# Turning double-precision weights into single precision: the lowest three fraction bits by ScalarE through PSUM, one VectorE operation in place of two, and a new written order

## The chip, the cores and the metric

The kernel runs on one core of one Trainium2 chip. The metric is the device time of one execution in microseconds. A core has five engines that work side by side, each through its own queue in order: TensorE (PE in the profile; its weight loads are PEld), VectorE (DVE), ScalarE (ACT), GpSimd (POOL) and SyncE (SP), which here starts most of the transfers.

## The reference, cut to what matters

Three layers follow one another. Attention keeps, for each query, the 32 largest of 576 scores. A dense layer multiplies by `w_in`, takes h cos(h), and multiplies by `w_out`. A layer of 8 experts sends each token to the expert with the largest logit.

```python
scores = scale * np.matmul(q, k.transpose(0, 1, 3, 2))     # 2 x 8 heads, 576 x 576
kth = np.partition(scores, -32, axis=-1)[..., -32:-31]
scores = np.where(scores >= kth, scores, -1e9)
attn = exp(scores - max); attn /= attn.sum + 1e-09
x = np.matmul(attn, v)                                      # as 1152 tokens x 512
h = x @ w_in;  x = (h * np.cos(h)) @ w_out                  # 512 x 2048, 2048 x 512
expert = argmax(x @ w_gate)                                 # 8 experts, capacity 288
out[i] = gate[i] * (relu(x[i] @ w1[expert]) @ w2[expert])
```

`w_in` and `w_out` come in double precision (their scale is a numpy double), all else in single precision. TensorE needs single precision, so the kernel builds the single-precision words itself from the two 32-bit halves of each double.

## The kernel before, in words

The program is a list of 3678 small operations. Each is registered with `P.op(engine, cost, function, r=..., w=...)`: the cost is a price in us that only the planner uses, `r` and `w` name the tiles read and written. `P.flex` registers an operation with two or three engines to choose from; the string `PICKS` holds the choice for the first 612 of them. `ORDER` is a written permutation of all 3678. The planner walks through it (`in_order`), gives every new tile a slot of its ring, and issues the instructions, so `ORDER` is the order of each engine's queue. Waits between engines come from the tiles that the instructions really touch; `r` and `w` only set what may be issued when.

Attention goes in 36 steps, 32 whole ones of 128 queries for a pair of heads and 4 of another shape. In a whole step TensorE computes the scores in two halves of 288 columns into the single PSUM buffer `S`; each half is copied to `Sp` in SBUF (`scores`, L665 on ScalarE or L666 on VectorE). The fold (`pair_chain`, L835) takes the elementwise maximum and minimum of the two halves, the second read from `S`, the first from `Sp`; then VectorE draws the largest eight three times from the maxima (L847, L850) and once from all (L854), the last one ending the step's list. `softmax` subtracts a penalty (L892), exponentiates (L895) and scales (L905 to L907); `products` transposes (copies L665, L666) and multiplies with the values.

The doubles lie as pairs of 32-bit words. `convert` handles them in 32 chunks of 128x512: 16 of `w_in`, 16 of `w_out`. A first pass (L692 on ScalarE, L693 on GpSimd) scales the upper word, read as a float, which moves the exponent. VectorE shifts it left by three (L697, L707) and puts in the top three bits of the lower word (L699, L709). The sign is put back by VectorE for the first three chunks (L702), and by a ScalarE sign (L706) and a GpSimd product (L712) for the other 29.

The dense layer takes token tiles as their steps end (`layer_in`, `cosine`, `product`, `layer_out`). The sums of `layer_out` for one token tile stand in a PSUM tile `x2`, a ring of two slots. `route` and `place` find each token's expert and slot, with operations of 8 or fewer elements a partition; `largest` tallies (L1217 to L1225) and counts doubtful decisions (L1235 to L1237). Last come the experts, on TensorE mostly, each weight rounded and its remainder subtracted (`weights2`).

Of the kernel before, what the change touches and what calls it, by code (L numbers as in the profile page):

```python
# [11 lines left out]
I32 = mybir.dt.int32  # L12
U32 = mybir.dt.uint32
# [26 lines left out]
SIGN = -2 ** 31  # L40
HALF_PI = 1.5707964
# [5 lines left out]
    "1000000000000000000000000000000010000000000000000200000000000000000000000000000110000100000001000100"  # L47
    "0010000000010000000000000100000000010100000000000100000002000000000210000000001001000010000000100000"
    "0000000000000000000022000100000110000002000000022000000022010000001000000010000001122000000010000101"
    "0011110001201110111111110000001010010000010000000101100000000000000000000010110101111101110100100101"  # L50
    "0101100000000111011101111101010000001000000000000000100110110111010000000110000000101001001000011011"
    "0001010000010101001011100100100110001111111101001010000000000101101000000010110101110011110110010001"
    "000000000000")
ORDER = [
# [490 lines left out]
def forward(ctx, lasting, tc, kq, vn, vs_, w_in, w_out, w_gate, w1, w2, out, paired):  # L545
# [125 lines left out]
    def convert(n):  # L671
# [9 lines left out]
        def half():  # L681
            return T[kt][:, 0]

        def full():
            return T[kf]
# [87 lines left out]
    ring("pt", "ps", [128, 512], F32, 2)  # L773
    ring("av", "ps", [128, 512], F32, 1, tag="av")
    ring("h", "pa", [128, 512], F32, 1)
    ring("x2", "ps", [128, 512], F32, 2)
    ring("xn", "xq", [128, 4, 128], F32, 2, tag="xl")

    def load_kq(s):
# [874 lines left out]
```

## Time and profile before

| | us |
|---|---|
| median of 3 runs | 663.94 (662.0 to 667.82) |
| the profiled execution | 664.33 |
| its span | 662.4 |
| busy in the span: TensorE | 583.6 (88%) |
| VectorE | 557.3 (84%) |
| ScalarE | 484.3 (73%) |
| GpSimd | 318.1 (48%) |

The span runs from the first to the last instruction of one execution. Busy time is the sum of the times in which an engine executes; register, branch and semaphore instructions don't count. The shares are averages over stages with different limits. The mean granted clock of TensorE is 0.963 of full speed.

### The profile page before, as it was taken

How to read it: one execution, taken by the hardware profiler on the slowest of the kernel's cores; microseconds unless marked ns; L12 is line 12 of the kernel's file. 1: busy time of each engine (PE TensorE's matmuls, PEld its weight loads, DVE VectorE, ACT ScalarE, POOL GpSimd, SP SyncE). 2: the span in 40 equal slices, each digit the busy share in tenths (PEclk: the TensorE clock that was granted, in tenths of full speed). 3: DMA queues.
4: the chain of work that ended last, by engine and by line, in shares of the span. 5: the costliest groups of instructions: out<-in, count | busy, mean ns of one | idle time of the engine just before them, and what ended most of it. 6: DMA issues, size and time to landing. Idle time of an engine off the chain costs nothing.

```text
span 662.4 us, 11583 instructions
## 1 busy us (share of the span) xinstructions
PE 583.6 (88%) x3808; PEld 452.8 (68%) x3808; DVE 557.3 (84%) x1541; ACT 484.3 (73%) x996; POOL 318.1 (48%) x406
## 2 busy tenths in 40 slices
PE   2256878888989999999999999999789999999994
PEld 0024665665447866778577688788468998889993
DVE  5999999999999999999999997556656688787782
ACT  3588798988997979979878787345336677777771
POOL 1557667777786887646666625045531010101111
PEclk9986689999999999999999999999879899999998
DMA  8756596822222243232121110242335587676750
GB/s 274 229 162 221 146 390 258 284 68 57 72 83 83 91 129 102 62 104 81 47 84 59 41 41 18 84 137 99 117 124 174 173 267 249 223 233 203 246 180 16
DMA packets 44613, 94.62 MB, mean 143 GB/s; under 512 B 7165, under 2 KB 11261, under 8 KB 44544
## 3 DMA queue, kind: packets, MB, share of 16 engines
q1 hardware_dynamic: 42800, 89.04, 41.2%
q0 software_dynamic: 1744, 4.76, 1.9%
q8 instruction: 32, 0.52, 0.3%
q14 instruction: 37, 0.30, 0.2%
HBM read 81.87 MB, written 12.69 MB: 143 GB/s over the span
## 4 chain that ended last, share of the span: by engine, by line
PE 41%; DVE 35%; issue 12%; ACT 6%; POOL 3%; DMA 1%; POOLq 0%; SPq 0%; DVEq 0%; ACTq 0%
DVE C L850 8%; DVE W L847 7%; PE yp L1503 6%; PE x L1109 5%; DVE C L835 4%; PE hp L1458 4%; PE x L1101 4%; DVE W L854 3%; PE h L1026 3%; DVE wt L709 3%; PE h L1028 2%; PE h L1027 2%; PE hp L1463 2%; PE av L936 2%; PE pt L922 2%
## 5 line engine op out<-in xcount | busy, mean ns | idle before, releaser
L892 POOL TENSOR_TENSOR Sp<-Sp,pen 128x576 f32<-128x576 f32 x62 | 82.6, 1333 | 29.5 <-ACT pen L888 27.2
L847 DVE MAX8 W<-C 128x8 f32<-128x288 f32 x216 | 93.9, 451 | 2.1
L850 DVE MATCH_REPLACE8 C<-W,C 128x288 f32<-128x288 f32 x216 | 94.7, 441 | 0.0
L807 PE MATMUL S<-kq 64*128 64x288 f32 x256 | 56.0, 519 | 33.4 <-DVE C L835 16.5
L1508 POOL DMA_INDIRECT out_dram<-ot,ti x16 | 16.1, 1004 | 140.1 <-ACT ot L1517 72.3
L1101 PE MATMUL x<-wo,hs 128*128 128x512 f32 x148 | 73.4, 606 | 1.6 <-POOL wo L712 0.8
L922 PE MATMUL pt<-ident,Sp 128*128 128x128 f32 x324 | 55.9, 294 | 16.1 <-ACT Sp L905 11.6
L922 PEld LDWEIGHTS pt<-ident,Sp 128*128 128x128 f32 x324 | 39.0, 148 | 43.3 <-ACT Sp L905 19.8
L888 ACT ACTIVATE pen<-Sp,tb 128x576 bf16<-128x576 f32 x72 | 55.4, 769 | 13.2 <-POOL tb L881 6.4
L807 PEld LDWEIGHTS S<-kq 64*128 64x128 f32 x256 | 22.1, 210 | 55.0 <-issue 30.2
L895 ACT ACTIVATE Sp<-Sp,tb 128x576 f32<-128x576 f32 x72 | 55.4, 771 | 5.3 <-POOL Sp L892 4.1
L1028 PE MATMUL h<-xh,wl 128*128 128x256 f32 x192 | 54.2, 282 | 0.0
L854 DVE MAX8 W<-C 128x8 f32<-128x576 f32 x72 | 52.7, 749 | 0.7
L665 ACT ACTIVATE Sp<-S 128x576 f32<-128x576 f32 x66 | 42.3, 641 | 14.7 <-PE S L807 9.3
L835 DVE TENSOR_TENSOR C<-S,Sp 128x576 f32<-128x576 f32 x64 | 47.5, 750 | 6.4 <-ACT Sp L665 4.4
L665 ACT ACTIVATE PT<-pt 128x384 f32<-128x384 f32 x89 | 41.6, 488 | 13.7 <-PE pt L922 10.7
L936 PE MATMUL av<-PT,v 128*64 128x128 f32 x320 | 45.6, 291 | 5.5 <-DVE xl L969 4.0
L936 PEld LDWEIGHTS av<-PT,v 128*64 128x64 f32 x320 | 36.5, 144 | 17.9 <-DVE xl L969 5.5
L938 PE MATMUL av<-PT,v 128*64 128x128 f32 x320 | 45.6, 291 | 1.8 <-DVE PT L666 1.2
L905 ACT ACTIVATE Sp<-Sp,sm 128x576 f32<-128x576 f32 x49 | 37.0, 769 | 4.8 <-DVE sm L900 4.6
L1463 PE MATMUL hp<-xgs,la 128*128 128x192 f32 (+2 forms) x160 | 40.2, 254 | 0.0
L1458 PE MATMUL hp<-xgs,wk 128*128 128x384 f32 x128 | 39.9, 374 | 0.0
(224 smaller groups left out, 1868.9 us busy)
## 6 DMA issues: line engine op xcount, KB each, us to landing
raw<-in_w_dram SPq DMA_DIRECT2D x64, 512.0 KB, 4.4
kq<-in_kq_dram SPq DMA_DIRECT2D x40, 288.0 KB, 3.4
v<-in_vn_dram SPq DMA_DIRECT2D x32, 320.0 KB, 3.4
wraw<-in_w_in_dram SPq DMA_DIRECT2D x16, 512.0 KB, 5.7
wraw<-in_w_out_dram SPq DMA_DIRECT2D x16, 512.0 KB, 4.1
xs<-z SPq DMA_DIRECT2D x1, 4680.0 KB
v<-in_vs_dram SPq DMA_DIRECT2D x8, 320.0 KB, 3.0
out_dram<-z SPq DMA_DIRECT2D x1, 2304.0 KB
```

Of the source, the lines that this page charges most:

```text
L665: P.flex([("act", act, lambda: ACT.activation(*args(), AF.Copy, scale=scale), False), ("dve", dve, lambda: DVE.tensor_scalar(*args(), scal ...
L807: PE.matmul(T[kp][:, a, 0:HS], t[p, S:S + 128], t[p, i * HS:(i + 1) * HS], start=True, stop=True)
L835: DVE.tensor_tensor(out=o[:, :, c:c + HS], in0=T["S", (s, 1)][:, :, 0:HS], in1=x[:, :, 0:HS], op=op)
L847: P.op("dve", 0.372, lambda r=r, i=i: DVE.max(T["W", s][:, i, LIST[r]:LIST[r] + 8], T["C", s][:, i, 0:HS]), r=[("C", s, i)], w=[("W", s, i)])
L850: P.op("dve", 0.42, lambda r=r, i=i: DVE.match_replace(T["C", s][:, i, 0:HS], T["W", s][:, i, LIST[r]:LIST[r] + 8], T["C", s][:, i, 0:HS], ...
L854: P.op("dve", 0.665, lambda i=i: DVE.max(T["W", s][:, i, 40:48], T["C", s][:, i, :]), r=[("C", s, i), ("C", s, 2 + i)], w=[("W", s, i)])
L892: eng.tensor_tensor(out=T["Sp", s][:, i, :], in0=T["Sp", s][:, i, :], in1=T[kp], op=OP.subtract)
L922: PE.transpose(T[kp][:, c * 128:(c + 1) * 128], P2[:, cc * 128:(cc + 1) * 128], ident)
L936: PE.matmul(o[0:64, 0:128], v[:, c * 64:(c + 1) * 64], chunk(c), start=(c == 0), stop=(c == 4), skip_group_check=True)
L1028: PE.matmul(o, lo, a, start=False, stop=(kc == 3), skip_group_check=True)
L1101: P.op("pe", 0.87, lambda f=f, a=a: PE.matmul(T["x2", t], T[kh][:, a:a + 128], T["wo", f], start=(f == 0), stop=(f == 15)), r=[kh, ("wo", ...
L1458: PE.matmul(o, hi_at(ka)[:, c:c + 128], x.rearrange("p a n -> p (a n)"), start=(kc == 0), stop=False, skip_group_check=True)
```

## The change

ScalarE gets a pass for each chunk that multiplies the lower word, read as an unsigned integer, by just under 2^-29, subtracts just under one half, and writes the result as an integer, 0 to 7, into PSUM. One VectorE operation shifts the scaled upper word and joins these bits to it, in place of two. The new tiles `lo` share the two slots of `x2`. The sign is handled as before.

```diff
+TOP3 = 2.0 ** -29 * (1 - 2.0 ** -21)
+HALF = 0.5 - 2.0 ** -21
...
+        kl = ("lo", n)
+        P.op("act", 0.5, lambda: ACT.activation(T[kl], T[kr][:, :, 0].bitcast(U32), AF.Copy, scale=TOP3, bias=-HALF), r=[kr],
+             w=[kl])
         P.flex([("act", 0.56, lambda: ACT.activation(half(), T[kr][:, :, 1].bitcast(F32), AF.Copy, scale=2.0 ** -112), False),
...
         if n < prm["mul"]:
-
-            P.op("dve", 0.34, port=True, fn=lambda: DVE.tensor_scalar(bits(full()), bits(half()), 3, None,
-                                                                      op0=OP.logical_shift_left), r=[kt], w=[kf])
-            P.op("dve", 0.60, port=True, fn=lambda: DVE.scalar_tensor_tensor(
-                bits(full()), T[kr][:, :, 0], 29, bits(full()), op0=OP.logical_shift_right, op1=OP.bitwise_or),
-                r=[kr], w=[kf])
+            P.op("dve", 0.62, port=False, fn=lambda: DVE.scalar_tensor_tensor(
+                bits(full()), bits(half()), 3, T[kl], op0=OP.logical_shift_left, op1=OP.bitwise_or),
+                r=[kt, kl], w=[kf])
...
         else:
             P.op("act", 0.56, lambda: ACT.activation(full(), T[kr][:, :, 1].bitcast(F32), AF.Sign), r=[kr], w=[kf])
-            P.op("dve", 0.34, port=True, fn=lambda: DVE.tensor_scalar(bits(half()), bits(half()), 3, None,
-                                                                      op0=OP.logical_shift_left), w=[kt])
-            P.op("dve", 0.60, port=True, fn=lambda: DVE.scalar_tensor_tensor(
-                bits(half()), T[kr][:, :, 0], 29, bits(half()), op0=OP.logical_shift_right,
-                op1=OP.bitwise_or), r=[kr], w=[kt])
+            P.op("dve", 0.62, port=False, fn=lambda: DVE.scalar_tensor_tensor(
+                bits(half()), bits(half()), 3, T[kl], op0=OP.logical_shift_left, op1=OP.bitwise_or),
+                r=[kl], w=[kt])
...
-    ring("x2", "ps", [128, 512], F32, 2)
+    ring("x2", "ps", [128, 512], F32, 2, tag="x2")
+    ring("lo", "ps", [128, 512], I32, 2, tag="x2")
...
-                P.op("dve", 0.69, lambda c=c, op=op: fold(c, op, 0), r=[("Sp", s, 0), ("S", (s, 1))], w=w, port=False)
+                P.op("dve", 0.69, lambda c=c, op=op: fold(c, op, 0), r=[("Sp", s, 0), ("Sp", s, 1), ("S", (s, 1))], w=w, port=False)
...
-        P.op("dve", 0.4, address, r=[kp, kx + (1,), ("pick", t)], w=[("slot", t)])
+        P.op("dve", 0.6, address, r=[kp, kx + (1,), ("pick", t)], w=[("slot", t)])
...
-        P.op("dve", 0.9 if paired else 0.3, tally, r=[kp, ("slot", 8)], w=[("counts", 0)])
+        P.op("dve", 2.9 if paired else 0.9, tally, r=[kp, ("slot", 8)], w=[("counts", 0)])
...
-        P.op("dve", 0.4, lambda: (DVE.tensor_scalar(edge, edge, 0.0, 0.0, op0=OP.is_gt, op1=OP.add, accum_out=doubts[:, 0:1]),
+        P.op("dve", 4.0, lambda: (DVE.tensor_scalar(edge, edge, 0.0, 0.0, op0=OP.is_gt, op1=OP.add, accum_out=doubts[:, 0:1]),
```

The fold's `r` now names the copy of the second half, so the planner may issue a fold only after that copy; the fold itself is the same. `address`, the tally and the doubts only get other prices. `PICKS` and `ORDER` are written anew, whole. Counted over the whole program, the new `PICKS` give:

| operation | engine: before to after |
|---|---|
| first pass of a chunk | ScalarE 25 to 11, GpSimd 7 to 21 |
| copy of scores | ScalarE 66 to 61, VectorE 6 to 11 |
| penalty subtraction | GpSimd 62 to 68, VectorE 10 to 4 |
| scaling of probabilities | ScalarE 49 to 40, VectorE 10 to 14, GpSimd 13 to 18 |
| copy of transposed probabilities | ScalarE 89 to 94, VectorE 19 to 14 |
| remainders of `w_in`, `w_out` (`split_w`, `split_wo`) | GpSimd 21 to 26, VectorE 5 to 0 |
| remainder `gl` in `product` | GpSimd 10 to 14, VectorE 8 to 4 |

In the new `ORDER` the steps come in the same sequence, 20 of the 32 chunks (before 18) are joined when step 5's list ends, and all 32 (before 31) when step 12's ends.

## Rows read from the trace of the kernel before

**Rows 1.** Busy time by stretch: length, PE, PEld, DVE, ACT, POOL, PEclk, DMA share, GB/s
```profile
0.00:167.90 167.90, 114.79 (x737) 77.36 (x738) 157.50 (x401) 133.98 (x249) 105.18 (x137) 0.92 0.63 209
100.00:150.00 50.00, 44.00 (x314) 31.03 (x314) 48.81 (x124) 46.17 (x88) 37.67 (x43) 1.00 0.57 199
167.90:406.90 239.00, 229.37 (x1635) 168.21 (x1635) 225.29 (x653) 201.28 (x380) 158.69 (x206) 1.00 0.24 73
406.90:600.00 193.10, 185.63 (x1139) 159.28 (x1135) 132.74 (x369) 112.39 (x276) 47.77 (x57) 0.96 0.50 167
```
**Rows 2.** Timeline of VectorE: start, duration; the end of step 13's list
```profile
167.15 0.75 DVE L854 MAX8 W<-C 128x8 f32<-128x576 f32 x1
```
**Rows 3.** Groups by line and form, VectorE, `convert`: busy us, mean ns, idle before
```profile
L709 DVE SCALAR_TENSOR_TENSOR wt<-wraw,wt 128x512 int32<-128x512 int32 x29 | 23.2, 810 | 0.0
...
L707 DVE TENSOR_SCALAR wt<-wt 128x512 int32<-128x512 int32 x29 | 17.1, 602 | 0.0
...
L699 DVE SCALAR_TENSOR_TENSOR ws<-wraw,ws 128x512 int32<-128x512 int32 x3 | 2.3, 777 | 0.0
...
L697 DVE TENSOR_SCALAR ws<-wt 128x512 int32<-128x512 int32 x3 | 1.3, 446 | 2.2 <-ACT wt L692 2.2
```
**Rows 4.** The same view, VectorE, the fold
```profile
L835 DVE TENSOR_TENSOR C<-S,Sp 128x576 f32<-128x576 f32 x64 | 47.5, 750 | 6.4 <-ACT Sp L665 4.4 <-PE S L807 0.3
...
L837 DVE TENSOR_TENSOR C<-S,Sp 128x288 f32<-128x288 f32 x16 | 6.8, 449 | 0.6 <-ACT Sp L665 0.4
```
**Rows 5.** Instructions on `wraw`: ns minimum/median/maximum, first and last start
```profile
L709 DVE SCALAR_TENSOR_TENSOR wt<-wraw,wt x29: 664/683/1754, 12.8 to 158.8; 128x512 int32<-128x512 int32 x29
L692 ACT ACTIVATE wt<-wraw x25: 643/666/815, 7.6 to 138.3; 128x512 f32<-128x512 f32 x25
```
**Rows 6.** Groups by line and form, ScalarE, copies out of PSUM
```profile
L665 ACT ACTIVATE Sp<-S 128x576 f32<-128x576 f32 x66 | 42.3, 641 | 14.7 <-PE S L807 9.3 <-DVE C L835 3.5 <-PE pt L922 1.4
...
L665 ACT ACTIVATE hs<-h 128x512 f32<-128x512 f32 x29 | 17.1, 589 | 9.2 <-PE h L1028 9.2
```
**Rows 7.** The same view: operations whose engine the picks change
```profile
L895 ACT ACTIVATE Sp<-Sp,tb 128x576 f32<-128x576 f32 x72 | 55.4, 771 | 5.3 <-POOL Sp L892 4.1 <-DVE Sp L892 1.0
...
L665 ACT ACTIVATE PT<-pt 128x384 f32<-128x384 f32 x89 | 41.6, 488 | 13.7 <-PE pt L922 10.7 <-PE av L938 2.7
...
L905 ACT ACTIVATE Sp<-Sp,sm 128x576 f32<-128x576 f32 x49 | 37.0, 769 | 4.8 <-DVE sm L900 4.6
...
L892 DVE TENSOR_TENSOR Sp<-Sp,pen 128x576 f32<-128x576 f32 x10 | 10.5, 1052 | 0.7 <-ACT pen L888 0.7
...
L906 DVE TENSOR_SCALAR Sp<-Sp,sm 128x576 f32<-128x576 f32 x10 | 9.5, 950 | 0.1
...
L693 POOL TENSOR_SCALAR wt<-wraw 128x512 f32<-128x512 f32 x7 | 5.3, 753 | 13.6 <-DMA wraw<-in_w_in_dram 9.5 <-DVE C L850 3.9
...
L666 DVE TENSOR_SCALAR Sp<-S 128x576 f32<-128x576 f32 x6 | 4.5, 744 | 3.8 <-PE S L807 3.8
```
**Rows 8.** Waits of VectorE: total us, times, longest us
```profile
DVE C L835 <- ACT Sp L665: 4.4, 11, 0.7
```
**Rows 9.** Timeline around one fold, all engines
```profile
106.94 0.76 PE L807 MATMUL S<-kq 64*128 64x288 f32 x4
...
107.80 0.64 ACT L665 ACTIVATE Sp<-S 128x576 f32<-128x576 f32 x1
...
108.47 0.76 DVE L835 TENSOR_TENSOR C<-S,Sp 128x576 f32<-128x576 f32 x1 [0.45 <-ACT Sp L665]
```
**Rows 10.** Timeline around 470 to 476 us, all engines
```profile
470.69 3.96 DVE L1237 TENSOR_TENSOR doubtb<-doubts 128x1 bf16<-128x1 f32 x1
...
470.87 3.77 POOL L657 TENSOR_TENSOR wl<-raw,wk 128x512 fp32r<-128x512 f32 x3
...
474.58 0.68 DVE L1085 TENSOR_TENSOR hs<-hs,ur 128x512 f32<-128x512 f32 x1
...
476.05 0.50 PE L1109 MATMUL x<-vh,gh 128*128 128x512 f32 x1 [2.98 <-ACT gh L660]
```

More of the change, by code (lines that the diff above doesn't have):

```diff
@@ L12 @@
 I32 = mybir.dt.int32
+U32 = mybir.dt.uint32
 U32 = mybir.dt.uint32
@@ L46 @@
 PICKS = (
[L47 to L53, printed above, removed]
-ORDER = [
[186 rows of a table removed]
+    "1100200000000000100000000000000020100000000000000200010000120000000100000000000010000010000000010000"
+    "0000000000000110101000000000000000000011000000000010100000100000000000001000200001002000010000200001"
+    "0000000000020000000002000000011000000002000000010000000021001000010000000000000000020011001022000010"
+    "0220001001210001110211111110111100001000110110011111111100000000100000000000111101110101011111110101"
+    "0101111100001111111101010111011101000000000001000000110011010010010000100100000000100111001011101001"
+    "1000000000100111110100101010000011111100011101011010000000100000001010000000010101010101010101110101"
+    "000010001000")
+ORDER = [
[186 rows of a table added]
 ]
```

372 rows, old and new, of the table ORDER are left out of this document.

## The prediction

> **What bounds the kernel now.** I first cut the span into stages and read how busy each engine is in each [rows 1]. The cut at 167.9 us is the end of the last candidate list of attention step 13 of 36 [rows 2]: by then all 32 weight chunks are converted, and everything that the change edits in `convert` lies before it. In that first stage VectorE is busy 157.5 of 167.9 us, TensorE only 114.8, ScalarE 134.0, GpSimd 105.2. VectorE sets the pace: its idle time is 10.4 us, most of it before the first data arrive. From 167.9 to the end of step 35 at 406.9 TensorE is busy 229.4 of 239.0 us and VectorE 225.3, and from there to 600 TensorE is busy 185.6 of 193.1, VectorE 132.7. So a microsecond taken from VectorE in the first stage can shift all that follows, because TensorE's later work stays the same and only starts earlier; one taken from VectorE after 168 us buys little. The question is therefore what the first stage becomes, and then a few us around 475.
>
> **The conversion.** Before, each chunk has on VectorE a shift (L707, or L697 for the first three) and a shift-and-or (L709, L699), besides the sign operation of three chunks, which stays. Their busy time is 17.1 + 23.2 + 1.3 + 2.3 = 43.9 us [rows 3]. Both leave; one join of 128x512 with one operand in PSUM comes. No row shows just that. The nearest is the fold, two inputs with one in PSUM: 0.750 us at 576 elements and 0.449 at 288 [rows 4], so 1.05 ns an element and 0.68 us at 512. The removed operation on SBUF alone has 0.664 at its fastest and 0.810 as its mean [rows 3, 5]. I take 0.68, since the fold has the same operands' places, with 0.66 and 0.81 as ends: 32 x 0.68 = 21.8, so VectorE loses 22.1 us (18.0 to 22.8). A second way to count gives less: at nearly undisturbed length (0.446, the mean of L697, and 0.683, the median of L709 [rows 3, 5]) the removed operations make 32 x 1.129 = 36.1 us, and the other 7.8 are time spent held up beside GpSimd. Should that holding-up pass to other VectorE operations, only 36.1 - 21.8 = 14.3 us are saved.
>
> The stretching shows at L709, whose longest took 1.754 us against a median of 0.683 [rows 5], and at the tiny L1237: 3.96 us for one element a partition, from 470.69 to 474.65, while GpSimd ran three subtractions from 470.87 to 474.64 [rows 10]. The Trainium skill (SBUF — State Buffer, section "SBUF: two separate sides") says that VectorE and GpSimd share a pair of SBUF ports which one instruction holds to its end, and that a VectorE operation with two SBUF inputs takes part in that. By this rule the join, with one SBUF input, stays at 0.68 beside GpSimd; without it, 0.81 and 18.0 us saved would be as likely.
>
> **ScalarE** gets 32 new passes that read every other word of the raw chunk, as L692 does (median 0.666 us [rows 5]), and write integers to PSUM. No row shows a write of ScalarE to PSUM; the ends are 0.59, the 512-element copy out of PSUM [rows 6], and 0.77, a scaling of 576 elements [rows 7]. I take 0.67: 21.4 us (18.9 to 24.6).
>
> **The picks** move work too. I counted, in the old and the new list, what stands ahead of step 13's end. VectorE: score copies 1 to 3 (+2 x 0.744), penalty subtractions 3 to 0 (-3 x 1.052), scalings 2 to 4 (+2 x 0.950) [rows 7]: +0.2. ScalarE: 14 first passes of chunks go to GpSimd (-14 x 0.666 = -9.3 [rows 5]), 6 scalings fewer (-6 x 0.769 = -4.6 [rows 7]), two exponentials and two copies of transposed probabilities stand later (-2 x 0.771 - 2 x 0.488 = -2.5 [rows 7]). With the 21.4 that is +5.0. GpSimd takes the 14 first passes (14 x 0.753 = 10.5 [rows 7]) and six softmax operations (a third of 3.77 each, as its subtractions [rows 10]: 7.5). That makes 123 us in the stage, so GpSimd keeps about a fifth of it as slack and is not the bound.
>
> **The first stage then.** VectorE needs 157.5 - 22.1 + 0.2 = 135.6 us; with the same 10.4 idle the stage would end at 146.0. ScalarE needs 134.0 + 5.0 = 139.0, and it starts at 7.6 [rows 5]. Its highest share in any 50 us was 46.17, or 92% [rows 1], since it waits in order for products and scalars of other engines. At 92%: 7.6 + 139.0 / 0.923 = 158.2. The later of the two decides: 158.2, a gain of 9.7 us. VectorE with the small saving of 14.3 us would end at 153.8, still ahead of it. So the cover that VectorE's relief needs is ScalarE's, and only half the relief comes through.
>
> **Later stages.** From 168 to 407 TensorE idles 9.6 of 239.0 us [rows 1], and the new lists leave its work as it is: I take 0, with 4 us either way for the new order. Around 475 TensorE stood 2.98 us for a rounded product of ScalarE [rows 10], which waited for the product L1085 behind L1237 in VectorE's queue. The new list puts that last product ahead of L1237, and gives the last remainder `gl` to GpSimd (1.26 us, a third of its 3.77, in place of VectorE's 0.68, taken as long as L1085 [rows 10]): a gain of 3.0 - 0.6 = 2.4, between 0 and 3. Repricing the tally and the doubts changes no instruction, so by itself it is worth nothing. Sum: -9.7 - 2.4 = -12.1 against the profiled execution's 664.3 us (span 662.4), which lies 0.4 above the median of the three runs: 652.2.
>
> **Rivals.** (1) VectorE's relief comes through whole: ScalarE runs at 98% as VectorE now does (157.5 of some 160). For it: no row says that ScalarE can't; against it: its many waits. The stage ends at 146.0, a gain of 21.9 + 2.4: 640.0. (2) The shared PSUM slots hold ScalarE. The bits' tiles use the ring `x2` of two slots, and from step 7 to step 13 one of them holds token tile 0's sums, so nine of the new passes must each wait for the join of the one before. With VectorE full, each may block ScalarE's queue (score copies and exponentials stand behind it) for one short operation and the join, 0.45 + 0.68 = 1.13 us [rows 4]: 10.2 us, in a stage where ScalarE is the later: 662.4. (3) On the slow side: the fold. It now also names the copy of the second score half, so in the new list all 32 whole-step folds stand behind that copy, 27 of them behind ScalarE; in the old one 9 did. That order costs a real wait: at 108.02 VectorE was free, the scores were in PSUM at 107.70, and the fold began at 108.47, right behind ScalarE's copy of 107.80 to 108.44 [rows 9]. The Trainium skill (PSUM — Partial Sum Buffer, section "PSUM bank collisions raise a hardware error") says that two engines may not read one bank at once, so a program has to put them in order; the trace agrees, with those 0.45 us. Eleven such waits made 4.4 us, 0.7 at the longest [rows 8]. At 0.4 each, 18 more cost 7 us, partly inside VectorE's slack. If ScalarE is so full that each fold waits for one earlier pass and the copy (0.77 + 0.64 = 1.41 us [rows 6, 7]), 27 x 1.41 - 4.4 = 33.7, less the 13.7 us that VectorE idles after 168: +20.0, 672. With two passes ahead it is 693. From about 1.4 us a fold this makes the kernel slower; I give 680 for the case.
>
> **How the numbers follow.** Forecast, 644 to 657: 0.48. Rival 1, 637 to 644: 0.20. Rival 2, or a gain eaten by fold waits of 0.4 us, 657 to 668: 0.24. Rival 3: 0.08. The range that holds eight in ten takes in both bounds of the first stage, 637 to 665. A change of less than 1% (6.6 us, 657.3 to 670.6) can't be told from none here: faster 0.68, within 0.24, slower 0.08.
>
> **What would show it.** In the profile of the changed kernel: the join near 0.68 us, 32 times; the new ScalarE pass near 0.67; step 13's last list ending near 158; ScalarE above 90% of 10 to 158 us and VectorE a few per cent lower than now; the stall at 475 gone; TensorE's idle time before 168 us shorter by some 10 us and the same after. I would be wrong if step 13 ends at 146 (ScalarE was never a bound) or beyond 165 (slots or folds), if folds wait over 1 us, or if TensorE turns out to idle after 170 us.

## The result, and the profile after

| | before | after |
|---|---|---|
| median, us | 664.18 (662.0 to 668.74, 6 runs) | 635.94 (634.24 to 636.73, 6 runs) |
| profiled execution; its span | 664.33; 662.4 | 635.66; 633.9 |

The ratio is 0.956, with a 95% interval of 0.952 to 0.959. The forecast was 652.2 with a range from 637: right in sign, and 16 us too high. Medians and ratios here and below are those of fast runs; one of fold_dep's four runs, at 703.97 us, was slow and is left out.

The span lost 28.5 us. Cut at the ends of the last lists of steps 13 and 35, as in [rows 1, 2], it lost 14.6 in the first stage (forecast 9.7), 6.4 in the middle one (forecast 0) and 7.5 behind it (forecast 2.4). Step 13 now ends with this row of VectorE's timeline (two lists of the step that follow without a gap, in one row; line numbers differ by a few between kernels, so L856 is the L854 of before):

```profile
151.90 1.40 DVE L856 MAX8 W<-C 128x8 f32<-128x576 f32 x2
```

Busy time of the changed kernel by stage, with the columns of [rows 1]:

```profile
0.00:153.30 153.30, 110.25 (x727) 73.89 (x727) 139.38 (x371) 134.19 (x253) 112.37 (x158) 0.92 0.67 227
153.30:385.90 232.60, 229.86 (x1657) 170.11 (x1653) 218.40 (x644) 201.50 (x384) 164.61 (x213) 1.00 0.25 77
385.90:633.90 248.00, 234.27 (x1431) 204.08 (x1429) 162.85 (x485) 149.10 (x371) 63.91 (x69) 0.97 0.52 169
```

In the first stage VectorE lost 18.1 us of work, ScalarE gained only 0.2 (forecast 5.0). In the middle TensorE's idle time fell from 9.6 to 2.7 us, at nearly the same busy time (229.4 and 229.9). Behind it TensorE's busy time fell by 5.2 us and its idle time by 2.3, against this row of the kernel before:

```profile
406.90:662.40 255.50, 239.46 (x1443) 207.19 (x1438) 174.56 (x488) 149.02 (x369) 54.27 (x63) 0.96 0.49 165
```

The new operations of the changed kernel (instructions on the tile `lo`: minimum, median, maximum in ns, as in [rows 5]):

```profile
L696 ACT ACTIVATE lo<-wraw x32: 612/634/742, 7.4 to 135.9; 128x512 int32<-128x512 uint32 x32
L710 DVE SCALAR_TENSOR_TENSOR wt<-wt,lo x29: 661/677/689, 13.7 to 136.7; 128x512 int32<-128x512 int32 x29
```

The join is what was forecast, 0.68 us, and never longer than 0.689, where the operation that it replaces went up to 1.754 [rows 5]. The fold waits for ScalarE's copy less than before, 3.1 us in 5 waits against 4.4 in 11 [rows 8] (waits of VectorE, whole span; L837 is the fold):

```profile
DVE C L837 <- ACT Sp L668: 3.1, 5, 0.9
```

### The profile page after: what moved, and what is told of

Its sections match the earlier page's. It is cut to its first block, busy times and chain, and to the rows that moved or that the text cites. A ratio compares the mean times of both kernels' runs of the same rounds, so it can differ in the third digit from the quotient of the medians.

```text
span 633.9 us, 11567 instructions
## 1 busy us (share of the span) xinstructions
PE 574.4 (91%) x3808; PEld 448.1 (71%) x3808; DVE 520.6 (82%) x1498; ACT 484.8 (76%) x1006; POOL 340.9 (54%) x439
## 4 chain that ended last, share of the span: by engine, by line
PE 61%; ACT 15%; DVE 14%; issue 7%; DMA 1%; POOL 1%; SPq 0%; POOLq 0%; DVEq 0%; ACTq 0%
PE yp L1505 9%; PE x L1111 7%; PE x L1103 6%; PE hp L1460 5%; PE av L938 4%; PE pt L924 4%; PE S L809 4%; PE h L1028 3%; PE hp L1465 3%; DVE C L852 3%; PE h L1030 3%; PE h L1029 3%; DVE W L849 3%; ACT Sp L897 2%; DVE C L837 2%
## 5 line engine op out<-in xcount | busy, mean ns | idle before, releaser
L894 POOL TENSOR_TENSOR Sp<-Sp,pen 128x576 f32<-128x576 f32 x68 | 88.5, 1302 | 36.0 <-ACT pen L890 35.4
L809 PE MATMUL S<-kq 64*128 64x288 f32 x256 | 55.7, 516 | 33.7 <-DVE C L837 19.7
L668 ACT ACTIVATE PT<-pt 128x384 f32<-128x384 f32 x94 | 43.9, 488 | 12.4 <-PE pt L924 12.0
L856 DVE MAX8 W<-C 128x8 f32<-128x576 f32 x72 | 52.8, 751 | 0.6
L837 DVE TENSOR_TENSOR C<-S,Sp 128x576 f32<-128x576 f32 x64 | 47.0, 749 | 5.0 <-ACT Sp L668 3.1
L938 PEld LDWEIGHTS av<-PT,v 128*64 128x64 f32 x320 | 36.9, 145 | 14.6 <-issue 4.1
L668 ACT ACTIVATE Sp<-S 128x576 f32<-128x576 f32 x61 | 39.4, 646 | 6.2 <-PE S L809 4.8
L1087 POOL TENSOR_TENSOR hs<-hs,ur 128x512 f32<-128x512 f32 x25 | 32.7, 1310 | 8.9 <-ACT ur L1078 8.8
```

Source lines behind the costliest of these rows:

```text
L668: P.flex([("act", act, lambda: ACT.activation(*args(), AF.Copy, scale=scale), False), ("dve", dve, lambda: DVE.tensor_scalar(*args(), scal ...
L809: PE.matmul(T[kp][:, a, 0:HS], t[p, S:S + 128], t[p, i * HS:(i + 1) * HS], start=True, stop=True)
L837: DVE.tensor_tensor(out=o[:, :, c:c + HS], in0=T["S", (s, 1)][:, :, 0:HS], in1=x[:, :, 0:HS], op=op)
L894: eng.tensor_tensor(out=T["Sp", s][:, i, :], in0=T["Sp", s][:, i, :], in1=T[kp], op=OP.subtract)
L938: PE.matmul(o[0:64, 0:128], v[:, c * 64:(c + 1) * 64], chunk(c), start=(c == 0), stop=(c == 4), skip_group_check=True)
```

## The experiments

Each was run beside the kernel before; the ratio is to its median there (664.2 to 666.7). The stages are cut as above, in the profiled execution of each.

| kernel | median us | ratio, 95% interval | to step 13 | 13 to 35 | rest |
|---|---|---|---|---|---|
| before | 664.18 | 1 | 167.9 | 239.0 | 255.5 |
| after | 635.94 | 0.952 to 0.959 | 153.3 | 232.6 | 248.0 |
| conv_alone | 706.57 | 1.057 to 1.071 | 179.7 | 266.8 | 258.5 |
| fold_dep | 694.90 | 1.034 to 1.047 | 172.7 | 266.3 | 257.2 |
| conv_oldfold | 666.73 | 0.998 to 1.005 | 170.1 | 239.1 | 253.3 |
| plan_alone | 667.47 | 1.002 to 1.007 | 185.6 | 230.2 | 250.9 |
| old_picks | 664.73 | 0.995 to 1.001 | 165.5 | 244.6 | 253.8 |
| fold_first | 643.88 | 0.961 to 0.971 | 156.0 | 236.4 | 249.1 |
| dve_twice | 657.44 | 0.985 to 0.993 | 171.0 | 232.6 | 248.7 |
| act_twice | 651.81 | 0.977 to 0.986 | 168.3 | 232.9 | 249.3 |
| passes_back | 638.13 | 0.955 to 0.965 | 155.3 | 232.6 | 247.4 |
| early_old | 643.84 | 0.965 to 0.974 | 160.8 | 232.7 | 248.3 |
| passes_pool | 633.70 | 0.947 to 0.956 | 151.1 | 232.6 | 248.5 |
| late_old | 652.60 | 0.977 to 0.986 | 151.8 | 244.8 | 253.4 |
| rem_old | 644.34 | 0.965 to 0.975 | 152.2 | 237.4 | 251.9 |
| soft_old | 647.64 | 0.971 to 0.980 | 151.9 | 244.3 | 249.7 |
| doubts_late | 665.86 | 0.998 to 1.004 | 169.7 | 239.0 | 255.4 |
| gl_pool | 661.43 | 0.992 to 0.999 | 169.1 | 239.0 | 251.3 |

### Which part of the change does it?

**conv_alone**: the changed code with the old lists.

```diff
 after.py
-ORDER, PICKS of the changed kernel
+ORDER, PICKS of the kernel before; each new pass ahead of its chunk's first pass
```

> The new conversion with the old order and the old picks: each new ScalarE pass stands right ahead of its chunk's first pass, the join where the shift-and-or stood. Theory 1 (the VectorE time that the conversion no longer takes is the gain): step 13's list ends near 150 us, and the kernel takes 640 to 648, most of the 28 us gained. Theory 2 (the new order and picks bring it, since the old order sends ScalarE the same first passes and 20 us more): step 13 ends at 160 or later and the kernel takes 655 to 664.

**plan_alone**: the old code with the new lists.

```diff
 before.py
-ORDER, PICKS of the kernel before
+ORDER, PICKS of the changed kernel; both old operations where the join stands
```

> The old conversion with the new order and the new picks: the shift stands right ahead of the shift-and-or, where the join stood, and no ScalarE pass writes PSUM. Theory 1: VectorE is as loaded as before, step 13 ends near 168 and the kernel takes 655 to 668, at most the few us of the stall near 475 gained. Theory 2: ScalarE is relieved by 14 first passes and 9 scalings, so that the kernel takes 640 to 648 without the new conversion.

Each half alone loses, 42 and 3 us; together they gain 28. conv_alone misses both theories: it lies 43 us above the upper end of the second. plan_alone is in theory 1's range in time, but its first stage is 18 us longer than that theory had it, and its middle one 8.8 shorter than before. The first stage of plan_alone holds 172.6 us of VectorE in 185.6, mostly because the conversion that it kept got longer. Its groups by line and form, to be laid beside L709 and L707 of [rows 3]:

```profile
L707 DVE SCALAR_TENSOR_TENSOR wt<-wraw,wt 128x512 int32<-128x512 int32 x29 | 30.0, 1035 | 1.0
L705 DVE TENSOR_SCALAR wt<-wt 128x512 int32<-128x512 int32 x29 | 20.6, 710 | 0.1
```

The same 58 instructions take 50.6 us in place of 40.3, while GpSimd runs 21 first passes in place of 7. Laid against GpSimd's rows in plan_alone's trace, the 13 shift-and-ors that ran beside no GpSimd instruction took 0.692 us on average, the 16 others 1.314. In the changed kernel the 4 joins of L710 beside none took 0.672, the 25 others 0.676. So the join lets GpSimd take work that made the old conversion longer.

The loss of conv_alone mixed two things, the conversion and the fold's new dependency, which moves 23 folds behind ScalarE's copy in the old order. Two runs take them apart.

**fold_dep**: the kernel before with the dependency.

```diff
-    fold(c, op, 0), r=[("Sp", s, 0), ("S", (s, 1))]
+    fold(c, op, 0), r=[("Sp", s, 0), ("Sp", s, 1), ("S", (s, 1))]
```

> The kernel before with one edit: the fold's list of reads names the copy of the second half too, so 23 of the 32 folds of whole steps are issued behind that copy instead of ahead of it. Conversion, order and picks are the old ones. Theory A (the dependency is the larger part of the 42 us that the conversion alone lost): each such fold waits about one pass and a copy of ScalarE (1.41 us), 23 x 1.41 = 32 us less some slack: 680 to 696 us. Theory B (it costs only where ScalarE is full, that is together with the new pass): folds wait 0.4 us each, 23 x 0.4 = 9 us at most: 664 to 673 us.

**conv_oldfold**: conv_alone without it.

```diff
-    fold(c, op, 0), r=[("Sp", s, 0), ("Sp", s, 1), ("S", (s, 1))]
+    fold(c, op, 0), r=[("Sp", s, 0), ("S", (s, 1))]
```

> The conversion of the changed kernel with the old order and the old picks, as in the run with the conversion alone, but the fold names only the copy of the first half again, so that the 23 folds which the old order has ahead of the second copy stay there. Theory A (ScalarE and VectorE both run almost without idle time): VectorE is relieved by 22 us, ScalarE's work in the first stage grows from 134.0 to 154.5 us, it starts at 7.6 and ends the stage at 162 to 166 instead of 167.9; the later stages stay as before: 657 to 664 us, folds waiting for ScalarE's copy under 6 us in total. Theory B (my prediction's share of 92%): 7.6 + 154.5 / 0.923 = 175 us for the stage, 671 us in all. Theory C (the new pass and the shared PSUM slots by themselves upset the old order, whatever the fold does): 690 us or more, as with the conversion alone, 706.

The dependency alone costs 28 us, theory A. Of the 33.8 us by which the profiled span is longer, 4.8 lie in the first stage and 27.3 between steps 13 and 35, where TensorE idles 28.2 us in place of 9.6 and its granted clock is 0.97 in place of 1.00. The waits of VectorE in fold_dep, against the 4.4 us of [rows 8]:

```profile
DVE C L835 <- ACT Sp L665: 44.1, 27, 3.5
```

The conversion without it is worth nothing, though VectorE is relieved by 19.7 us. The first stage of conv_oldfold:

```profile
0.00:170.10 170.10, 113.97 (x735) 76.57 (x736) 137.78 (x369) 149.36 (x281) 96.71 (x137) 0.91 0.60 205
```

VectorE is busy 137.8 of 170.1 us: it is no longer what holds the stage. ScalarE went from 134.0 to 149.4, and the forecast's rule (ScalarE's start, 5.8 here, and its work at 92%) gives 5.8 + 149.4 / 0.923 = 167.6; measured, 170.1 lies between theories A and B, as the time does. Its folds waited 18.4 us in all, three times what A allowed. The dependency costs 28 us without the new pass and 40 with it (conv_alone against conv_oldfold); in conv_alone the folds waited 57.2 us in all, up to 4.1.

**old_picks**: the changed kernel, old choice of engines.

```diff
 after.py
-PICKS of the changed kernel
+PICKS of the kernel before
```

> The changed kernel, its conversion and its order, with the old choice of engines: 14 first passes of chunks come back from GpSimd to ScalarE (14 x 0.666 = 9.3 us), some 9 scalings too (6 of them in the first stage, 4.6 us), and 10 remainders and 6 penalty subtractions come back from GpSimd to VectorE, most of them after the first stage. Theory A (ScalarE and VectorE both set the pace of the first stage, VectorE that of the middle one): step 13 ends 10 to 14 us later than 153.3, the middle stage gets 4 to 7 us longer than 232.6: 650 to 657 us. Theory B (the order matters and the picks don't): 636 to 640 us.

The first stage comes back by 12.2 us, as theory A had it; but the middle by 12.0, where it had 4 to 7, and the rest by 5.8, so that the time lies 8 us above its range. The picks carry all of the gain in this order. New picks in the old order were not tried, so what the order contributes by itself stays open.

**fold_first**: in the changed kernel, the second copy right behind its step's folds, in 32 steps.

```diff
-    ..., copy of the second half, ..., fold (max), fold (min)
+    ..., fold (max), fold (min), copy of the second half
-    r=[("Sp", s, 0), ("Sp", s, 1), ("S", (s, 1))]
+    r=[("Sp", s, 0), ("S", (s, 1))]
```

> The changed kernel with the fold naming only the first copy again and, in the order, the copy of the second half moved right behind the second fold of its step. All else is the changed kernel. Theory A (in the changed kernel the copy is done before VectorE comes to the fold, 3.1 us of waits in all, so the dependency costs nothing and moving the copy back can only make the buffer S free later): TensorE's scores wait longer for S, first stage 0 to 8 us longer, 636 to 644 us. Theory B (the dependency still costs about 0.4 us a fold hidden in other waits): 626 to 634 us.

Theory A, at its upper end: 8 us slower. In an order that has the copy done in time the folds wait little for it (3.1 us in the changed kernel), where the dependency cost 28 us in the old one. Moving the copy back behind the folds loses; the dependency with the order left alone was not tried.

### What holds the first stage?

**dve_twice** issues the join twice, **act_twice** the new pass twice; nothing else changes.

```diff
+    DVE.scalar_tensor_tensor(bits(half()), bits(half()), 0, T[kl], op0=OP.logical_shift_left, op1=OP.bitwise_or)
```
```diff
+    ACT.activation(T[kl], T[kr][:, :, 0].bitcast(U32), AF.Copy, scale=TOP3, bias=-HALF)
```

> The changed kernel with the join issued twice, the second time with a shift by zero, so that the result is the same: 32 more VectorE operations of 0.68 us, 21.8 us, order and picks as in the changed kernel. If VectorE still sets the pace of the first stage, step 13 ends 18 to 22 us later and the kernel takes 650 to 658. If ScalarE sets it, as the prediction had it, step 13 ends under 10 us later and the kernel takes 637 to 646.

> The changed kernel with the new ScalarE pass issued twice into the same PSUM tile: 32 more ScalarE passes of 0.64 us, 20.4 us. If ScalarE sets the pace of the first stage, step 13 ends 18 to 22 us later and the kernel takes 650 to 658. If VectorE sets it and ScalarE's 19 us of idle time take the passes in, step 13 ends under 10 us later and the kernel takes 637 to 646.

21.9 us more on VectorE (161.25 busy) make the stage 17.7 us longer, 19.1 us more on ScalarE (153.33 busy) 15.0. Both engines hold it, at four fifths of full slope each in these two profiled executions. By the medians VectorE's slope is steeper: 21.5 us for the joins, 15.9 for the passes; the profiled execution of dve_twice, 654.09, was its fastest.

**passes_back** and **passes_pool** move first passes of chunks only, **early_old** the other 25 old choices ahead of step 13's end.

```diff
-first passes: ScalarE 11, GpSimd 21
+passes_back:  ScalarE 25, GpSimd 7
+passes_pool:  ScalarE 0, GpSimd 32
```
```diff
-softmax, copies, rounding up to step 13's end: new PICKS
+early_old: old PICKS there (25 differ), first passes as in the changed kernel
```

> The changed kernel with the first passes of the chunks on their old engines: 25 on ScalarE and 7 on GpSimd in place of 11 and 21; conversion, order and all other picks are the changed kernel's. Theory A (ScalarE sets the end of the first stage, at some 92% of its time; a pass takes 0.56 us of a full queue, as the 17.8 us show that 32 doubled passes added): ScalarE's busy time there grows from 134.2 to 142, 7.6 + 142 / 0.923 = 161.5 in place of 153.3, the middle stage stays at 232.6 us and the end as it is: 642 to 646 us. Theory B (the first stage is VectorE's alone, or the order's): 635 to 638 us.

> The changed kernel with all 32 first passes of the chunks on GpSimd, 11 more than now. Theory A: ScalarE's busy time in the first stage falls from 134.2 to 128, its end by that to 7.6 + 128 / 0.923 = 146; then VectorE decides, 139.4 busy + 10.4 idle = 149.8, 3.5 us earlier than now: 631 to 634 us. Theory B (GpSimd, with 112.4 + 7.3 = 120 us of work in 150, in order, is the next to hold the chunks up): 636 to 645 us.

> The changed kernel with the old choice of engines up to step 13's last list, but not for the first passes of the chunks: 25 operations differ; ScalarE gets 15 and loses 5, some 6 us more work in the first stage, VectorE gets 7 and loses 9. Theory A (additive: all old choices made the first stage 12.2 us longer, the first passes alone 2.0): 644 to 647 us. Theory B (it takes both to fill ScalarE): 636 to 640 us.

passes_back is a miss for theory A: 7.2 us more of ScalarE cost 2.0 us. Its first stage, and that of early_old:

```profile
0.00:155.30 155.30, 109.57 (x727) 73.17 (x727) 138.82 (x371) 141.40 (x267) 104.45 (x144) 0.98 0.66 224
```
```profile
0.00:160.80 160.80, 113.24 (x728) 75.78 (x729) 138.81 (x368) 139.94 (x263) 105.86 (x151) 0.92 0.64 216
```

early_old comes out 0.2 us below theory A's range; its first stage is 7.5 us longer, where a plain sum (12.2 less 2.0) would have 10.2. It has less of ScalarE than passes_back, the same of VectorE, and ends 5.5 us later. So what counts is not the amount alone but what kind of operation moves. A likely reason, not tested by itself: first passes hang on nothing but a transfer, while softmax operations stand in a chain from one engine to the next. ScalarE's share is no constant: over the whole stage it was 87% in early_old, 87.5% in the changed kernel, 91% in passes_back and act_twice. passes_pool, in theory A's range, ends the stage 2.2 us earlier and has the lowest median of all, 633.70; its interval overlaps that of the changed kernel, so whether it is faster isn't settled.

### The middle stage

**late_old** has the old choices behind step 13's end (134 operations), **rem_old** only the eleven remainders among them, **soft_old** all but those.

```diff
-PICKS of the changed kernel behind step 13's last list
+late_old: old PICKS there
+rem_old:  old PICKS there for wl, vl (L659, L660) of w_in, w_out and gl of product
+soft_old: old PICKS there for all others
```

> The changed kernel with the old choice of engines for everything that stands behind step 13's last list in its order, and the new one ahead of it (134 operations differ: the remainders of w_in, w_out and the product that went to GpSimd come back to VectorE, with copies, scalings and products). Theory A (the later choices are what shortened the middle stage and the end): step 13 at 153.3 as in the changed kernel, the middle stage 7 to 12 us longer than 232.6, the end 3 to 6 us longer, 646 to 654 us. Theory B (the middle stage got shorter because the order changed, or because the first stage left work behind in a better state): 636 to 639 us.

> The changed kernel with only the remainders of w_in, w_out and of the dense layer's product on their old engines: 10 come back from GpSimd to VectorE and one goes the other way, all of them behind step 13. Theory A (these carry the middle stage: VectorE's 225.3 of 239.0 us there, of which the ten remainders are some 7): about two thirds of the 17 us that the run with all later choices lost, 645 to 650 us, middle stage 239 to 242. Theory B (the copies, scalings and penalty subtractions carry it): 636 to 641 us, middle stage 233 to 236.

> The changed kernel with the old choice of engines behind step 13's last list for all but those eleven remainders (123 operations). Theory A of the run with the remainders: 638 to 643 us here. Theory B: 645 to 650 us. If both this and the run with the remainders lose little (under 4 us each), the loss of 17 us comes only when both are together, that is when VectorE is full.

late_old came out in theory A's range, with the middle 12.2 us longer. Of its parts, soft_old falls where theory B had it, and rem_old between the two theories: the remainders cost 4.8 us in the middle, the other 123 choices 11.7, so the two are not a sum. All six kernels with the new later choices in the new order (the changed one, dve_twice, act_twice, passes_back, passes_pool, early_old) have 232.6 to 232.9 there, whatever their first stage was, and plan_alone, without the new conversion, has 230.2: this gain comes with the new lists, whichever conversion stands there; late_old shows that within the new order it needs the later picks. In soft_old TensorE waits where it waits in old_picks too (waits of TensorE in soft_old, 153 to 393 us):

```profile
PE pt L924 <- ACT Sp L907: 3.5, 6, 1.0
PE av L938 <- DVE xl L971: 1.2, 2, 0.8
```

These are ends of softmax chains on ScalarE and VectorE. The changed kernel has one such wait over half a microsecond there, of 0.9.

### The stall around 475

**doubts_late** moves the count of doubts, in the kernel before.

```diff
 ORDER of the kernel before
-..., doubts, last product, ..., copy xr of tile 8, ...
+..., last product, ..., doubts, copy xr of tile 8, ...
```

> The kernel before with one edit in the order: the count of doubts (VectorE, 3.96 us at 470.69) moves from ahead of the last product of the dense layer to behind it, just ahead of the copy that follows. Theory A (the stall of 2.98 us and the clock that falls with it, 0.81 in 473 to 500 and 0.93 in 500 to 550, make most of the 7.5 us by which the last part got shorter): 657 to 661 us. Theory B (my prediction's 2 to 3 us, the clock being set by other things): 661 to 663 us. Theory C (the stall moves to another wait): 664 us.

Theory C: no gain. The timeline of doubts_late, the rows of VectorE and GpSimd, shows why, beside [rows 10]:

```profile
471.04 1.67 POOL L659 TENSOR_SCALAR wk<-raw 128x512 fp32r<-128x512 f32 x2
...
472.16 4.86 DVE L1083 TENSOR_TENSOR hs<-hs,ur 128x512 f32<-128x512 f32 x1
...
472.68 3.78 POOL L655 TENSOR_TENSOR wl<-raw,wk 128x512 fp32r<-128x512 f32 x3
```

Now it is the product, 0.68 us by itself, that takes 4.86 beside the same three subtractions, while the count takes 0.16. The count was not the cause: either of these two operations, each with two SBUF inputs, is held when it stands there.

**gl_pool**: one pick, in the kernel before.

```diff
-PICKS[547] = "0"   # gl of the last product: VectorE
+PICKS[547] = "1"   # GpSimd, ahead of the three subtractions in its queue
```

> The kernel before with one pick changed: the last remainder of the dense layer's product goes to GpSimd, where it stands ahead of the three subtractions of 470.87 to 474.64 and waits for the last product by way of its rounding. So the three can't run beside the count of doubts or beside that product. Theory A (those three lengthen whatever VectorE runs beside them, 3.96 us for one element, 4.86 us for the product when the count was moved behind it): the count takes 0.2 us, the product 0.7, the stall of 2.98 us goes to under 1, and with it the lower clock behind it: 657 to 661 us, the part after step 35 at 248 to 251 us instead of 255.5. Theory B (the stall moves once more): 663 to 666 us.

Theory A in its mechanism, and 0.4 us above its range in time. The three now stand behind a remainder that waits for the last product by way of its rounding, and run when VectorE is past. VectorE and GpSimd in gl_pool's timeline:

```profile
471.87 0.22 DVE L1237 TENSOR_TENSOR doubtb<-doubts 128x1 bf16<-128x1 f32 x1
472.01 0.68 DVE L1085 TENSOR_TENSOR hs<-hs,ur 128x512 f32<-128x512 f32 x1
...
473.52 1.29 POOL L657 TENSOR_TENSOR gl<-hs,gh 128x512 fp32r<-128x512 f32 x1 [1.44 <-ACT gh L660]
474.77 3.79 POOL L657 TENSOR_TENSOR wl<-raw,wk 128x512 fp32r<-128x512 f32 x3
```

The part behind step 35 falls from 255.5 to 251.3, so this one choice is worth 4.2 of the 7.5 us in the profiled executions (3.4 by the medians). The lower clock, which theory A expected to go with the stall, stayed: 0.81 in 473 to 500 us in both kernels. rem_old agrees from the other side. With its remainders back on VectorE, the last one among them, the three subtractions run early again and hold the remainder before it, 0.69 us by itself; TensorE waits 3.0 us for that, and the part is 3.9 longer. VectorE and GpSimd in rem_old's timeline:

```profile
451.19 3.74 POOL L660 TENSOR_TENSOR wl<-raw,wk 128x512 fp32r<-128x512 f32 x3
451.29 4.21 DVE L659 TENSOR_TENSOR gl<-hs,gh 128x512 fp32r<-128x512 f32 x1 [2.00 <-POOL gh L664]
```

## Why the prediction missed, step by step

**The step that failed** is the one on the later stages: "the new lists leave its work as it is: I take 0", and 2.4 us for the stall. It holds 11.5 of the 16.4 us by which the forecast gain was too small, 6.4 in the middle stage and 5.1 behind it. The profile had the room in plain sight: 9.6 us of TensorE's idle time [rows 1], with VectorE at 225.3 of 239.0. I read TensorE at 96% as the end of the matter. I had counted the picks for the first stage only. In the new order the later ones decide there (late_old, soft_old, rem_old): with them TensorE waits less for the ends of softmax chains, and 6.9 of the 9.6 us went. What the order gives by itself stays open.

**The stall** was sized at 2.4 and measured 4.2 (gl_pool). I had named the pick that removes it and netted its price, but thought that moving the product ahead of the count was what counted; doubts_late shows that to be worth nothing. Most of the other 3.3 us shows in the granted clock, which I had not priced. These rows of the kernel before and of the changed one, with the columns of [rows 1], begin equally far behind step 35, the stall of 2.98 us left out (93.1 and 90.1 us):

```profile
500.00:550.00 50.00, 49.94 (x299) 45.90 (x299) 36.10 (x109) 35.57 (x100) 4.49 (x4) 0.93 0.65 213
476.00:526.00 50.00, 49.92 (x319) 45.89 (x319) 40.00 (x119) 35.60 (x100) 5.09 (x5) 1.00 0.71 232
```

TensorE is busy throughout in both, but a part of the first stretch ran at 1.2 GHz in place of 2.4, and 20 fewer matmuls were done. gl_pool, without the stall, still has 0.93 and 302 matmuls in 498 to 548 us. From its 302 to the changed kernel's 319 are about 2.7 us of TensorE at the rate of the second row (an estimate), so that much of the 3.3 comes with the clock. What in the new lists kept the clock up stays open.

**The first stage** had a term that was mis-sized, for the other 4.9 us, and a rule that was right only in part. GpSimd came out at 112.4 us in place of 123, and not as the bound, as forecast. The forecast was 7.6 + 139.0 / 0.923 = 158.2; with ScalarE's measured 134.2 the same sum gives 153.0, and the stage ended at 153.3. The term of +5.0 for the new passes less the picks came out at +0.2. Summed over all groups of ScalarE in the stage the rows grew from 152.5 to 156.4 us, by 3.9, near the forecast; but rows of neighbours overlap, and busy time counts a moment once. ScalarE in the changed kernel's timeline:

```profile
108.92 0.24 ACT L897 ACTIVATION_READ_ACCUMULATOR Sp<-Sp,tb 128x1 f32 x1
109.02 0.70 ACT L696 ACTIVATE lo<-wraw 128x512 int32<-128x512 uint32 x1
109.59 0.69 ACT L668 ACTIVATE Sp<-S 128x576 f32<-128x576 f32 x1
```

The new pass ends at 109.72, the copy behind it starts at 109.59. Here each row hides 0.13 or 0.14 us of its length under the next; summed over the stage, what is hidden grew from 18.5 to 22.2 us, which is the difference between +3.9 and +0.2. The Trainium skill (Perfetto Trace Analysis, section "Optimizing Scalar/DVE Operations") says that the write-acknowledgement half of an instruction's overhead overlaps with the next instruction; the trace agrees, in direction.

That the sum came out at 153.0 is partly luck. The forecast took 92% for ScalarE's highest share in any 50 us of the kernel before, but other stretches there show more, 94% in this one:

```profile
90.00:140.00 50.00, 44.97 (x330) 33.51 (x332) 48.74 (x132) 47.10 (x86) 36.50 (x41) 0.97 0.74 263
```

At 94% the sum with 134.2 gives 150.1, where VectorE's (139.4 and the 10.4 idle) gives 149.8; the stage took 153.3, with VectorE idle for 13.9. Over the runs the rule that the later engine decides, at 92%, holds for dve_twice (171.7 by VectorE, measured 171.0) and comes near for early_old (159.2, measured 160.8), but is 5 us too high for act_twice (173.7, measured 168.3) and passes_back (160.8, measured 155.3).

**The conversion on VectorE** was right: 19.4 + 2.0 = 21.4 us of joins against 21.8 forecast. The stage's VectorE lost 18.1 in place of 21.9; the sign operation of the first three chunks, two SBUF inputs, is 1.044 us long where it was 0.681, and two more score copies, which the forecast had, and a product, which it had not, add 2.2. The new pass took 0.639 against 0.67.

**The rivals.** VectorE's relief came through for 14.6 of 18.1 us, not whole and not by half: dve_twice and act_twice show that both engines hold the stage. Rival 1's sum did not fit its own condition: 139.0 us of ScalarE do not go into the 138.4 between its start and 146.0, and at 98% it gives 149.4. The PSUM slots (rival 2) cost 1.1 us in two waits. The fold (rival 3) was priced nearly right and wrongly placed: in fold_dep 27 folds wait, 1.63 us each against 1.41 forecast, but only in an order that was not made for it, and most of the cost lies behind step 13.

## What to carry to other kernels

An engine that is busy 96% of a stage still has its last 4% to give, and moved operations of other engines can free them: count what picks and order move in every stage, not only where the edit stands. When work goes from a full engine to another, look at what that one must give away in turn; here the conversion alone, with the old fold, was worth nothing, and it took the new order and picks to make it pay. When a VectorE operation takes several times its usual length, look at what GpSimd runs beside it: here moving that helped, and moving the operation did not.

## What the hardware showed that I had not expected

A VectorE operation with two SBUF inputs can be held not for one GpSimd instruction but for a whole run of them: the product in doubts_late began at 472.16, while GpSimd ran two roundings until 472.71, and ended at 477.02, 0.56 us behind the last of the three subtractions that followed without a gap. The Trainium skill (SBUF — State Buffer, section "SBUF: two separate sides") says that the shared ports are held by one instruction to its end; the trace shows GpSimd's next instructions ahead of the waiting VectorE one each time. Operations with one SBUF input are not free of it altogether: the old shift, with one, took 0.446 in its shortest group and 0.602 in the other [rows 3], and 0.710 in plan_alone, where GpSimd had more to do, while the join with its second input in PSUM stayed at 0.661 to 0.689 beside the same GpSimd.
